# Attention and two expert layers in one kernel: q, k and w3 read from host-transposed copies, phi made for two heads at once

## The chip, the cores and the metric

The kernel runs on one core of a Trainium2 chip. The metric is the device time of one execution in microseconds (us), lower is better. Five engines take part: PE (matrix products and transposes; its weight loads are listed as PEld), DVE (vector operations, and the only one besides ACT that reads PE's results from PSUM here), ACT (activations and copies), POOL (GpSimd, elementwise on SBUF) and SP, which only issues DMAs. Each engine runs its instructions in a fixed order and waits on semaphores.

## The reference

```
scores = q @ k.T / sqrt(64), causal;  local = softmax(scores) @ v       # 2 x 8 heads, 576 tokens, D = 64
phi(x) = where(x > 0, x, exp(x) - 1) + 1
mem    = (phi(q) @ M_prev) / (phi(q) . z_prev + 1e-6)
x      = g * mem + (1 - g) * local,  g = sigmoid(beta) by head          # 1152 tokens x 512
h      = (x @ w1) * (x @ w2) @ w3;   x2 = h @ w_out                     # 512 -> 1024 -> 1024 -> 512
out    = sum over 4 experts e of p[:, e] * (relu(x2 @ e_w1[e]) @ e_w2[e])
```

The inputs w1, w2, w3 and w_out of the first layer are float64 and the rest float32.

## The kernel before

Every float32 operand of a product is split into a high part (rounded to 12 significant bits) and a low part (the rest), each carried by one float32r pass. Where nothing else is said a product takes three passes (`PASSES`, high-low, low-high, high-high). The high part is a copy (ACT `copy`, or `hi_pool` on POOL, L74), the low part a subtraction (`lo_pool` on POOL, L77, or `lo_dve` on DVE, L80).

The work has three parts in time. **Attention**: 16 heads in slots numbered from -1. In slot n the program emits stage z of head n+3, stage t of head n+2, stage a of head n+1 and stage b of head n, and between them "fills": the conversion of w_out, then W = w3 @ w_out in 16 units (`w_unit`, slots 3 to 10.5), then h of the first batch in 16 units (`b0`, slots 10.5 to 15), then its product with W (`c_unit`, slot 15). Each step has a place in its slot (`Z_AT`, `T_AT`, `A_AT`, `B_AT`), and a scheduler that knows modelled costs settles from this program the fixed order of each engine's instructions. **Second batch**: the same two products for the tokens of batch 1. **Experts**: four experts, each two products with a ReLU between them.

The stages of a head:

- z (`stage_z`): q, k and v lie with tokens on partitions, 5 tiles of up to 120 tokens. phi(q) is made (ACT `ex`, `phi`; DVE L165), multiplied by z and summed (DVE L169, L171), the norm is inverted and multiplied in (L173, L177). q, k, v and phi are each split on POOL into `qs`, `ks`, `vs`, `ps`, M into `ms`.
- t (`stage_t`): PE transposes `qs`, `ks` and `ps`, 15 transposes a head (L222, L229), ACT and DVE copy them out of PSUM to T = [(high; low), tokens] and pT (L223, L230, L231), and two DMAs (L232, L233) make `kTs`, which is k with the halves swapped, (low; high).
- a (`stage_a`): scores in two passes over 128 rows, [qh; ql] against [kl; kh] and against [kh; kl], then mask, row minimum and exponential (DVE L255, ACT L261), and the weights are scaled by the gate over the row sum (L300 to L306).
- b (`stage_b`): PE transposes the weights (`pt`, L341), ACT and DVE split them into `ph` and `pl`, and PE sums M's term (one pass, L359) and the products with v (L364).

For w3, `w_conv` turns 128 x 512 float64 words into float32 on ACT and DVE (`from64`, L100 to L105), and `w_trans` transposes the tile on PE (four transposes `w3p`, L425), copies the high part on ACT and subtracts the low part on DVE (`w3T`, L426, L427). All loads are issued by SP, in order.

## Time and profile before

| | before |
|---|---|
| device time, median of 3 runs | 798.97 us (798.64 to 801.09) |
| span of the profiled execution, first to last instruction | 798.1 us |
| PE busy | 750.8 us (94%), 4352 instructions |
| DVE busy | 396.9 us (50%), 838 instructions |
| ACT busy | 283.0 us (35%), 671 instructions |
| POOL busy | 354.5 us (44%), 423 instructions |
| DMA packets | 69176, of which 38272 under 512 B |

The span is the profile's own time; it leaves out what lies before the first and behind the last instruction, and is 0.9 us under the median of the runs. A share of busy time is an average over the three parts of the program, which have different limits, so the rows below are taken by part. "Idle before" is the time that an engine waited in front of a group, with the instruction whose end released it.

### The profile page before, as it was taken

How to read it: one execution, taken by the hardware profiler on the slowest of the kernel's cores; microseconds unless marked ns; L12 is line 12 of the kernel's file. 1: busy time of each engine (PE TensorE's matmuls, PEld its weight loads, DVE VectorE, ACT ScalarE, POOL GpSimd, SP SyncE). 2: the span in 40 equal slices, each digit the busy share in tenths (PEclk: the TensorE clock that was granted, in tenths of full speed). 3: DMA queues.
4: the chain of work that ended last, by engine and by line, in shares of the span. 5: the costliest groups of instructions: out<-in, count | busy, mean ns of one | idle time of the engine just before them, and what ended most of it. 6: DMA issues, size and time to landing. Idle time of an engine off the chain costs nothing.

```text
span 798.1 us, 11693 instructions
## 1 busy us (share of the span) xinstructions
PE 750.8 (94%) x4352; PEld 668.4 (84%) x4352; DVE 396.9 (50%) x838; ACT 283.0 (35%) x671; POOL 354.5 (44%) x423
## 2 busy tenths in 40 slices
PE   2698998999899999899999999999999999999997
PEld 2486887889898999799988988889888898888986
DVE  4998999899999953665321211212112122121211
ACT  3877777676675643344220101201012010020100
POOL 6889377478798526722392018500194001500000
PEclk9857999899999999999999999999999999999999
DMA  6554545444433322431141004200042000201010
GB/s 144 159 144 140 147 124 144 127 121 124 129 104 103 109 65 93 159 106 54 41 131 41 1 1 132 79 1 1 1 132 79 1 1 1 67 0 40 14 40 26
DMA packets 69176, 62.41 MB, mean 78 GB/s; under 512 B 38272, under 2 KB 54656, under 8 KB 69120
## 3 DMA queue, kind: packets, MB, share of 16 engines
q1 hardware_dynamic: 69120, 61.68, 27.3%
q8 instruction: 34, 0.56, 0.3%
q14 instruction: 22, 0.18, 0.1%
...
## 4 chain that ended last, share of the span: by engine, by line
PE 68%; DVE 12%; DMA 8%; POOL 7%; issue 3%; ACT 2%; SPq 0%; DVEq 0%; POOLq 0%; ACTq 0%
PE d L653 25%; PE o L670 25%; PE ab L488 5%; PE c L550 4%; DMA wr<-in_moe_w_dram 3%; PE wacc L434 2%; DMA wor<-in_moe_w_out_dram 2%; PE xv L364 2%; POOL P L306 2%; PE sc L252 2%; PE pt L341 2%; DVE tu L102 1%; DVE P L255 1%; DVE tf L105 1%; DMA w3r<-in_moe_w_dram 1%
## 5 line engine op out<-in xcount | busy, mean ns | idle before, releaser
L670 PE MATMUL o<-el,he 128*128 128x512 f32 x864 | 200.9, 392 | 0.0
L670 PEld LDWEIGHTS o<-el,he 128*128 128x128 f32 x864 | 161.8, 188 | 36.1
L659 ACT ACTIVATE he<-d 128x512 fp32r<-128x512 f32 (+2 forms) x96 | 47.2, 491 | 342.1 <-PE d L653 339.6
L74 POOL TENSOR_SCALAR el<-rel 128x512 fp32r<-128x512 f32 x64 | 40.3, 636 | 210.9 <-PE d L653 186.4
L660 DVE SCALAR_TENSOR_TENSOR he<-d,he 128x512 fp32r<-128x512 f32 (+2 forms) x96 | 53.4, 557 | 147.2 <-ACT he L659 147.2
L488 PE MATMUL ab<-xT,ws 128*128 128x288 f32 x768 | 115.6, 301 | 2.9 <-DVE asb L537 1.5
L653 PE MATMUL d<-x2b,el 128*128 128x384 f32 (+1 forms) x768 | 113.8, 309 | 0.0
L653 PEld LDWEIGHTS d<-x2b,el 128*128 128x128 f32 x768 | 113.2, 189 | 0.7
L488 PEld LDWEIGHTS ab<-xT,ws 128*128 128x128 f32 x768 | 107.4, 192 | 4.5 <-DVE W L80 0.9
L653 PE MATMUL d<-x2a,el 128*128 128x512 f32 x384 | 89.6, 394 | 0.0
L653 PEld LDWEIGHTS d<-x2a,el 128*128 128x128 f32 x384 | 72.0, 188 | 16.9
L77 POOL TENSOR_TENSOR el<-rel,el 128x512 fp32r<-128x512 f32 x64 | 83.0, 1311 | 1.6
L679 DVE SCALAR_TENSOR_TENSOR acc<-o,pr,acc 128x512 f32<-128x512 f32 x27 | 20.3, 751 | 125.3 <-PE o L670 125.3
L550 PE MATMUL c<-hT,W 128*128 128x288 f32 x384 | 57.2, 298 | 3.9 <-DVE hT L80 3.7
L306 POOL TENSOR_SCALAR P<-P,sm 120x120 f32<-120x120 f32 (+4 forms) x71 | 55.1, 790 | 9.0 <-DVE sm L301 9.0
L550 PEld LDWEIGHTS c<-hT,W 128*128 128x128 f32 x384 | 52.4, 188 | 5.1 <-DVE hT L80 4.7
L434 PE MATMUL wacc<-wo,w3T 128*128 128x512 f32 x192 | 54.8, 420 | 0.0
L261 ACT ACTIVATE P<-P,mn 120x120 f32<-120x120 f32 (+4 forms) x80 | 46.7, 585 | 13.4 <-DVE mn L255 13.2
L341 PE MATMUL pt<-identF,P 114*120 114x114 f32 (+1 forms) x240 | 42.7, 287 | 5.2 <-DVE pl L80 2.9
L434 PEld LDWEIGHTS wacc<-wo,w3T 128*128 128x128 f32 x192 | 36.6, 201 | 6.7
L252 PE MATMUL sc<-kTs,T 128*120 128x120 f32 (+2 forms) x96 | 35.6, 380 | 4.7 <-DMA kTs<-T 3.1
L80 DVE TENSOR_TENSOR pl<-pt,ph 120x456 fp32r<-120x456 f32 (+1 forms) x64 | 37.4, 596 | 1.8 <-ACT ph L345 1.7
(112 smaller groups left out, 1059.2 us busy)
## 6 DMA issues: line engine op xcount, KB each, us to landing
...
```

The source lines that it names most:

```text
L77: nc.gpsimd.tensor_sub(dst, src, r32(hi))
L252: nc.tensor.matmul(ps_ap, lhsT=T[:, 0, q0[i] : q0[i] + RP], rhs=rhs, start=(m == 0), stop=(m == 1))
L261: nc.scalar.activation(Pt[i], Pt[i], AF.Exp, bias=mn[:, i : i + 1], scale=-1.0, accum_out=sm[:, i : i + 1])
L306: nc.gpsimd.tensor_scalar(out=Pt[i], in0=Pt[i], scalar1=sm[:, i : i + 1], scalar2=1.0, op0=ALU.mult, op1=ALU.mult)
L341: nc.tensor.transpose(pt[:, o - c0 : o - c0 + rows[i]], Pt[i][0 : rows[i], q0[j] : q0[j] + RP], identF[0 : rows[i], 0 : rows[i]],)
L434: nc.tensor.matmul(wacc[t], lhsT=w3T[u][:, a, c * P : (c + 1) * P], rhs=wo[4 * g + c][:, bb, :], start=(g == 0 and c == 0 and x == 0), sto ...
L488: nc.tensor.matmul(ps[:, 0:HS], lhsT=self.ws[u][:, wi, kk, :], rhs=xT[b, kk][:, xi, a * HS : (a + 1) * HS], start=(n == 0), stop=(n == 3 * ...
L550: nc.tensor.matmul(st["ps"][:, 0:HS], lhsT=Wt[kk][:, wi, d * P : (d + 1) * P], rhs=hT[kk][:, xi, a * HS : (a + 1) * HS], start=(kk == 0 an ...
L653: nc.tensor.matmul(ps, lhsT=ew1[m // 4 * 4 + kk][:, wi, m % 4 * P : (m % 4 + 1) * P], rhs=rhs[:, xi, :], start=(n == 0), stop=(n == 3 * KD ...
L659: nc.scalar.activation(ht[:, 0, :], ps, AF.Relu)
L660: nc.vector.scalar_tensor_tensor(out=ht[:, 1, :], in0=ps, scalar=0.0, in1=r32(ht[:, 0, :]), op0=ALU.max, op1=ALU.subtract,)
L670: nc.tensor.matmul(po, lhsT=hs[kk][:, xi, tt * P : (tt + 1) * P], rhs=ew2[kk][:, wi, :], start=(n == 0), stop=(n == 3 * KF - 1),)
```

## The change

The host passes transposed copies of q, k and w3 (`qT`, `kT`, `moe_w3T`), and q itself as before for phi. `load_head` reads qT and kT twice each, into the upper and the lower 64 partitions. `stage_h` makes of them T = (qh; ql) and K = two tiles, (kh; kh) and (kl; kl): the high parts by ACT copies, the low parts by POOL subtractions. The scores are still two passes of 128 rows, T against (kl; kl) and T against (kh; kh). Stages z and t and the DMAs to `kTs` are gone, and a head is loaded one slot later than before.

phi is made for two heads at once (`stage_pa`, `stage_pb`) on 120 x 640 elements. The product with z moves from DVE to POOL. phi is transposed in float32, both heads side by side, in 5 transposes for two heads, and split after it, the high part by ACT and the low part by DVE. The split of M is padded with zeros to 128 rows, and M's term takes two passes (high and low of phi) where it took one.

w3's tiles are split straight after the conversion, the high part by ACT and the low part by POOL. In `b0` the high part of w1 and w2 moves from POOL to ACT. The scaling of the last tile of weights is on ACT for all heads, where POOL did 7 of 16. The diff, cut to its core:

```diff
-Z_AT = (0.01, 0.15, 0.4, 0.45, 0.6, 0.75, 0.77)
-T_AT = (0.05, 0.06, 0.07, 0.08)
+PA_AT = (0.03, 0.2, 0.45, 0.6)
+PB_AT = (0.12, 0.15, 0.72)
+H_AT = (0.02, 0.1, 0.14, 0.75)
...
+    ms2 = [A1.tile([P, 2, 2 * D], F32R, name=f"ms{i}") for i in range(2)]
+    for t in ms2:
+        nc.gpsimd.memset(r32(t), 0.0)
+    def load_pair(p):
+        b, h = divmod(2 * p, H)
+        qn = A1.tile([RP, NQ, 2, D], F32, tag="qn", name=f"qn{p}")
+        for x in range(2):
+            src = q[b, h + x]
+            nc.sync.dma_start(out=qn[:, :, x, :], in_=bass.AP(src.tensor, src.offset, [[D, RP], [R * D, NQ], [1, D]]))
+        z = A1.tile([P, 2 * D], F32, tag="z", name=f"z{p}")
+        nc.sync.dma_start(
+            out=z, in_=z_prev[b, h : h + 2].rearrange("h d -> (h d)").unsqueeze(0).to_broadcast([P, 2 * D])
+        )
+        mr = A1.tile([P, D], F32, tag="mr", name=f"mr{p}")
+        nc.sync.dma_start(out=mr, in_=M_prev[b, h : h + 2].rearrange("h d e -> (h d) e"))
+        pair_t[p] = {"q": qn, "z": z, "m": mr}
...
+        for nm, src in (("q", qT), ("k", kT)):
+            t = A1.tile([P, S], F32, tag=f"{nm}d", name=f"{nm}d{n}")
+            for x in range(2):
+                nc.sync.dma_start(out=t[x * D : (x + 1) * D, :], in_=src[b, h])
...
+        t = A2.tile([RP, NQ, D], F32, tag="vr", name=f"vr{n}")
+        x = v[b, h]
+        nc.sync.dma_start(out=t, in_=bass.AP(x.tensor, x.offset, [[D, RP], [R * D, NQ], [1, D]]))
+        raw_t[n] = (*ts, t)
...
+    def stage_pa(p):
+        if p >= B * H // 2:
+            return []
+        st = pair_t[p]
+        h = 2 * p % H
+        def phi_a():
+            st["ex"] = ex = st["q"]
+            st["phi"] = phi = A1.tile([RP, NQ, 2, D], F32, tag="phi", name=f"phi{p}")
+            nc.scalar.activation(phi, st["q"], AF.Relu)
+            nc.scalar.activation(ex, st["q"], AF.Exp)
+            nc.vector.scalar_tensor_tensor(out=phi, in0=ex, scalar=1.0, in1=phi, op0=ALU.min, op1=ALU.add)
+        def phi_b():
+            ex, phi = (st[x].rearrange("p n h d -> p n (h d)") for x in ("ex", "phi"))
+            nc.gpsimd.tensor_mul(ex, phi, st["z"][0:RP].unsqueeze(1).to_broadcast([RP, NQ, 2 * D]))
+            m = ms2[p % 2]
+            for x in range(2):
+                o = slice(x * D, (x + 1) * D)
+                hi_pool(m[o, x, 0:D], st["m"][o, :])
+                lo_pool(m[o, x, D:], st["m"][o, :], m[o, x, 0:D])
+        def phi_c():
+            st["nrm"] = nrm = A1.tile([RP, NQ, 2], F32, tag="nrm", name=f"nrm{p}")
+            nc.vector.reduce_sum(out=nrm, in_=st["ex"], axis=AX.X)
+            nc.vector.scalar_tensor_tensor(
+                out=nrm, in0=nrm, scalar=1e-6, in1=gm[0:RP, h : h + 2].unsqueeze(1).to_broadcast([RP, NQ, 2]),
+                op0=ALU.add, op1=ALU.mult,
+            )
+            nc.vector.reciprocal(nrm, nrm)
+        def phi_d():
+            phi = st["phi"]
+            nc.vector.tensor_mul(phi, phi, st["nrm"].unsqueeze(3).to_broadcast([RP, NQ, 2, D]))
+        return [*zip(PA_AT, (phi_a, phi_b, phi_c, phi_d))]
+    q0 = [R * i for i in range(NQ)]
+    widths = [x + RP for x in q0]
+    rows = [R] * (NQ - 1) + [RP]
+    def stage_pb(p):
+        if p >= B * H // 2:
+            return []
+        st = pair_t.pop(p)
+        pT = A2.tile([P, 2, S], F32R, tag="pT", name=f"pT{p}")
+        pT_t[2 * p] = pT_t[2 * p + 1] = pT
+        def trans(c0, c1):
+            def f():
+                t0, t1 = q0[c0], q0[c1 - 1] + rows[c1 - 1]
+                ps = psQ.tile([P, 512], F32, tag="Q", name=f"tp{c0}_{p}")[:, 0 : t1 - t0]
+                for c in range(c0, c1):
+                    w = rows[c]
+                    nc.tensor.transpose(
+                        ps[:, q0[c] - t0 : q0[c] - t0 + w], st["phi"][0:w, c].rearrange("p h d -> p (h d)"),
+                        identF[0:w, 0:w],
+                    )
+                nc.scalar.copy(pT[:, 0, t0:t1], ps)
+                lo_dve(pT[:, 1, t0:t1], ps, pT[:, 0, t0:t1])
+            return f
+        return [*zip(PB_AT, (trans(0, NQ - 1), trans(NQ - 1, NQ)))]
+    def stage_h(n):
+        if n >= B * H:
+            return []
+        qd, kd, vr = raw_t.pop(n)
+        T = A2.tile([P, S], F32R, tag="T", name=f"T{n}")
+        K = A2.tile([P, 2, S], F32R, tag="K", name=f"K{n}")
+        vs = A2.tile([RP, NQ, 2 * D], F32R, tag="vs", name=f"vs{n}")
+        split_t[n] = T, K, vs
+        def fq():
+            nc.scalar.copy(T, qd)
+            lo_pool(T[D : 2 * D, :], qd[D : 2 * D, :], T[D : 2 * D, :])
+        def fk():
+            nc.scalar.copy(K[:, 0, :], kd)
+            lo_pool(K[:, 1, :], kd, K[:, 0, :])
+        def fv():
+            hi_pool(vs[:, :, 0:D], vr)
+            lo_pool(vs[:, :, D:], vr, vs[:, :, 0:D])
+        def nothing():
+            pass
+        return [*zip(H_AT, (fk, fq, nothing, fv))]
...
-                rhs = T[:, 1, k0:k1] if m else kTs[:, k0:k1]
-                nc.tensor.matmul(ps_ap, lhsT=T[:, 0, q0[i] : q0[i] + RP], rhs=rhs, start=(m == 0), stop=(m == 1))
+                nc.tensor.matmul(
+                    ps_ap, lhsT=T[:, q0[i] : q0[i] + RP], rhs=K[:, 1 - m, k0:k1], start=(m == 0), stop=(m == 1)
+                )
...
-            nc.scalar.activation(sm, sm, AF.Identity, bias=gle[0:RP, h : h + 1], scale=gl[0:RP, h : h + 1])
+            nc.vector.tensor_scalar(
+                out=sm, in0=sm, scalar1=1e-9, scalar2=gl[0:RP, h : h + 1], op0=ALU.add, op1=ALU.mult
+            )
             nc.vector.reciprocal(sm, sm)
             for i in range(NQ):
-                if i == NQ - 1 and n <= H:
+                if i == NQ - 1:
...
+        Pt, vs = prob_t.pop(n)
+        pT, ms = pT_t.pop(n), ms2[n // 2 % 2][:, n % 2, :]
...
-                nc.tensor.matmul(xv, lhsT=ms, rhs=pT[:, a0:a1], start=True, stop=False)
+                for x in range(2):
+                    nc.tensor.matmul(xv, lhsT=ms, rhs=pT[:, x, a0:a1], start=(x == 0), stop=False)
...
-        steps = stage_z(n + 3) + stage_t(n + 2) + stage_a(n + 1)
+        steps = stage_h(n + 2) + stage_a(n + 1)
+        steps += stage_pa(n // 2 + 1) if n % 2 == 0 else stage_pb((n + 1) // 2)
...
+            out=r.rearrange("p c f two -> p c (f two)"),
+            in_=w3T[g * 512 : (g + 1) * 512, t * 2 * P : (t + 1) * 2 * P].rearrange("(c p) f -> p c f", p=P),
         )
...
-        ps = psM.tile([P, 512], F32, tag="M0", name=f"w3p{u}", bufs=1)
-        for c in range(4):
-            nc.tensor.transpose(ps[:, c * P : (c + 1) * P], f[:, c * P : (c + 1) * P], identF)
-        nc.scalar.copy(w3T[u][:, 0, :], ps)
-        lo_dve(w3T[u][:, 1, :], ps, w3T[u][:, 0, :])
+        f = from64(raw3.pop(u), pf, f"l3{u}")
+        w3s[u] = pf.tile([P, 2, 4, P], F32R, tag="ws", name=f"w3s{u}")
+        nc.scalar.copy(w3s[u][:, 0], f)
+        lo_pool(w3s[u][:, 1], f, w3s[u][:, 0])
...
+    load_pair(0)
...
-    for st, n in ((stage_z, 0), (stage_t, 0), (stage_z, 1)):
+    for st, n in ((stage_h, 0), (stage_pa, 0)):
...
-    b0 = BUnits(0, hi_pool, lo_dve)
+    b0 = BUnits(0, nc.scalar.copy, lo_dve)
...
-        if n + 4 < B * H:
-            load_head(n + 4)
+        if n + 3 < B * H:
+            load_head(n + 3)
+        if n % 2 == 1 and (n + 3) // 2 < B * H // 2:
+            load_pair((n + 3) // 2)
...
+    inputs["qT"] = inputs["q"].transpose(0, 1, 3, 2)
+    inputs["kT"] = inputs["k"].transpose(0, 1, 3, 2)
+    inputs["moe_w3T"] = inputs["moe_w3"].T```

On PE, at the start of the program (`tq`, `tk`, `tr`, `tp` are the transposes of q, k, their last 120 tokens and phi; `sc` the scores; the number behind a name tells tiles apart). Before:

```order
L222 MATMUL tq_192<-identR,qs_173 128x114 x4
L222 MATMUL tk_198<-identR,ks_176 128x114 x4
L229 MATMUL tr_204<-identR,qs_173 128x120
L229 MATMUL tr_204<-identR,ks_176 128x120
L229 MATMUL tr_204<-identR,ps_180 128x120
L222 MATMUL tp_212<-identR,ps_180 128x114 x4
L222 MATMUL tq_274<-identR,qs_228 128x114 x4
L222 MATMUL tk_280<-identR,ks_231 128x114 x4
L252 MATMUL sc_0_308<-kTs_191,T_189 120x120
L252 MATMUL sc_0_308<-T_189 120x120
```

and of the change, the same place:

```order
L273 MATMUL sc_0_219<-K_144,T_143 120x120 x2
L273 MATMUL sc_0_219<-K_144,T_143 120x234 x2
L273 MATMUL sc_0_228<-K_144,T_143 120x348 x2
L273 MATMUL sc_0_228<-K_144,T_143 120x64 x2
L273 MATMUL sc_0_236<-K_144,T_143 120x462 x2
L273 MATMUL sc_0_241<-K_144,T_143 120x512 x2
L223 MATMUL tp_0_208<-identF,phi_152 128x114 x4
L273 MATMUL sc_1_326<-K_194,T_193 120x120 x2
```

The 23 transposes that stood ahead of the first scores are gone, and the transposes of phi stand behind them.

On POOL, between the scaling of the weights of heads 4 and 5, where the units of W run (`xT` is the split of attention's result, `w3s` that of w3's tiles). Before:

```order
L77 TENSOR_TENSOR vs_903<-vr_550,vs_903 120x5x64
L74 TENSOR_SCALAR qs_1305<-qr_919 120x5x64
L74 TENSOR_SCALAR ks_1317<-kr_921 120x5x64
L74 TENSOR_SCALAR xT_1_71<-xraw_761 128x576
L77 TENSOR_TENSOR qs_1305<-qr_919,qs_1305 120x5x64
L77 TENSOR_TENSOR ks_1317<-kr_921,ks_1317 120x5x64
L77 TENSOR_TENSOR xT_1_71<-xraw_761,xT_1_71 128x576
L74 TENSOR_SCALAR ms_1165<-mr_744 128x64
L77 TENSOR_TENSOR ms_1165<-mr_744,ms_1165 128x64
L74 TENSOR_SCALAR ps_1350<-phi_1218 120x5x64
L77 TENSOR_TENSOR ps_1350<-phi_1218,ps_1350 120x5x64
```

and of the change, the same place:

```order
L79 TENSOR_TENSOR w3s_774<-tf_l_768,w3s_774 128x512
L79 TENSOR_TENSOR w3s_832<-tf_l_826,w3s_832 128x512
L76 TENSOR_SCALAR vs_742<-vr_583 120x5x64
L76 TENSOR_SCALAR xT_1_69<-xraw_597 128x576
L79 TENSOR_TENSOR vs_742<-vr_583,vs_742 120x5x64
L79 TENSOR_TENSOR xT_1_69<-xraw_597,xT_1_69 128x576
L76 TENSOR_SCALAR ms_106<-mr_1144 64x64
L79 TENSOR_TENSOR K_1147<-kd_957,K_1147 128x576
L79 TENSOR_TENSOR ms_106<-mr_1144,ms_106 64x64
L79 TENSOR_TENSOR T_1146<-qd_954,T_1146 64x576
L79 TENSOR_TENSOR w3s_900<-tf_l_894,w3s_900 128x512
L79 TENSOR_TENSOR w3s_951<-tf_l_945,w3s_951 128x512
```

The splits of q, k and phi have left POOL's order, and the low parts of q, k and four tiles of w3 stand in it, each a subtraction of two SBUF tiles.

## Rows read from the trace of the kernel before

**Rows 1.** Busy by stretch: start:end, length, PE, PEld, DVE, ACT, POOL busy (count), clock, DMA, GB/s.
```profile
0.00:20.00 20.00, 5.46 (x28) 4.35 (x29) 8.98 (x20) 7.51 (x16) 13.32 (x28) 1.00 0.66 144
20.00:71.00 51.00, 38.84 (x178) 31.07 (x177) 47.02 (x119) 40.09 (x100) 44.42 (x52) 0.72 0.60 162
71.00:178.00 107.00, 102.20 (x622) 88.60 (x621) 99.06 (x233) 78.49 (x190) 67.96 (x96) 0.94 0.47 127
178.00:278.00 100.00, 94.05 (x705) 90.33 (x704) 97.32 (x227) 66.25 (x174) 80.88 (x100) 0.97 0.40 113
278.00:300.00 22.00, 22.00 (x170) 22.00 (x169) 13.30 (x28) 9.84 (x23) 4.97 (x7) 1.00 0.24 73
300.00:394.00 94.00, 88.32 (x648) 86.15 (x647) 48.73 (x78) 33.70 (x74) 41.91 (x37) 1.00 0.27 88
394.00:798.00 404.00, 399.97 (x2014) 345.94 (x2012) 82.45 (x137) 47.16 (x96) 101.05 (x108) 1.00 0.14 41
```

**Rows 2.** DVE groups, 0 to 300 us: busy us, mean ns of one, idle before.
```profile
L80 DVE TENSOR_TENSOR w3T<-w3p,w3T 128x512 fp32r<-128x512 f32 x16 | 10.8, 675 | 1.2 <-ACT w3T L426 1.1
L169 DVE TENSOR_TENSOR ex<-phi,z 120x320 f32<-120x320 f32 x16 | 10.5, 657 | 1.7 <-DMA z<-in_z_prev_dram 1.6
L230 DVE CAST T<-tr 128x240 fp32r<-128x240 f32 x16 | 6.3, 392 | 3.1 <-PE tr L229 3.1
L231 DVE CAST pT<-tr 128x120 fp32r<-128x120 f32 x9 | 2.4, 268 | 0.0
L80 DVE TENSOR_TENSOR pl<-pt,ph 120x456 fp32r<-120x456 f32 (+1 forms) x64 | 37.4, 596 | 1.8 <-ACT ph L345 1.7
L173 DVE RECIPROCAL nrm<-nrm 120x5 f32<-120x5 f32 x16 | 2.9, 178 | 0.9 <-ACT nrm L172 0.9
```

**Rows 3.** Timeline of DVE, 163 to 171 us: start us, us.
```profile
163.77 0.68 DVE L102 SCALAR_TENSOR_TENSOR tu<-tf,tu 128x512 uint32<-128x512 uint32 x1
164.37 0.48 DVE L171 TENSOR_REDUCE nrm<-ex 120x5 f32<-120x320 f32 x1
...
168.67 1.54 DVE L102 SCALAR_TENSOR_TENSOR tu<-tf,tu 128x512 uint32<-128x512 uint32 x1
```

**Rows 4.** Timeline of POOL, 160 to 200 us.
```profile
168.23 1.44 POOL L77 TENSOR_TENSOR xT<-xraw,xT 128x576 fp32r<-128x576 f32 x1
```

**Rows 5.** Busy on tile qs, 0 to 300 us: PE, PEld, POOL, clock, DMA, GB/s.
```profile
0.00:300.00 300.00, 13.41 (x80) 10.23 (x80) 25.66 (x32) 0.92 0.47 125
```

**Rows 6.** The same for tile ks.
```profile
0.00:300.00 300.00, 12.99 (x80) 10.48 (x80) 27.55 (x32) 0.92 0.47 125
```

**Rows 7.** The same for tile ps.
```profile
0.00:300.00 300.00, 12.85 (x80) 9.79 (x80) 25.91 (x32) 0.92 0.47 125
```

**Rows 8.** POOL groups, 0 to 300 us.
```profile
L74 POOL TENSOR_SCALAR ws<-tf 128x512 fp32r<-128x512 f32 x16 | 12.2, 764 | 13.8 <-PE ab L488 5.2 <-DVE pl L80 4.4 <-PE tr L229 2.8
L77 POOL TENSOR_TENSOR wo<-tf_wo,wo 128x512 fp32r<-128x512 f32 x8 | 11.6, 1445 | 1.1 <-ACT wo L403 1.1
```

**Rows 9.** Timeline of PE at full clock, 86 to 91 us.
```profile
86.69 0.60 PE L425 MATMUL w3p<-identF,tf_l 128*128 128x128 f32 x4
87.05 2.32 PE L434 MATMUL wacc<-wo,w3T 128*128 128x512 f32 x9
89.21 0.45 PE L222 MATMUL tq<-identR,qs 114*128 114x114 f32 x4
89.50 0.59 PE L341 MATMUL pt<-identF,P 120*120 120x120 f32 x4
89.85 0.35 PE L364 MATMUL xv<-pl,vs 114*128 114x228 f32 x1
90.04 0.22 PE L364 MATMUL xv<-ph,vs 114*128 114x114 f32 x1
```

**Rows 10.** Busy by stretch around a fall of the clock, columns as in the first group.
```profile
136.00:140.00 4.00, 1.48 (x8) 1.19 (x8) 4.00 (x8) 2.38 (x6) 3.36 (x4) 0.74 0.45 91
140.00:144.00 4.00, 4.00 (x10) 3.12 (x10) 4.00 (x10) 1.62 (x4) 2.17 (x5) 0.50 0.75 203
```

More of the change, by code (lines that the diff above doesn't have):

```diff
@@ L42 @@
     w2: bass.AP,
-    w3: bass.AP,
+    w3T: bass.AP,
     w_out: bass.AP,
@@ L52 @@
     NT, DM = out.shape
-    w1, w2, w3, w_out = (t.bitcast(U32) for t in (w1, w2, w3, w_out))
-    DF = w3.shape[0]
+    w1, w2, w3T, w_out = (t.bitcast(U32) for t in (w1, w2, w3T, w_out))
+    DF = w3T.shape[0]
     E = e_w1.shape[0]
@@ L395 @@
     wo = [po.tile([P, 2, DM], F32R, tag=f"o{c}", name=f"wo{c}") for c in range(KF)]
[L396 removed]
+    raw3, w3s, wacc = {}, {}, {}
     def wo_unit(c):
```

110 lines of the change are left out of this document (13 added, 97 removed).

## The prediction

> **What bounds the kernel now.** I read first the busy time by stretch [rows 1], then DVE's groups [rows 2], then the order in time on DVE, POOL and PE around single instructions [rows 3, 4, 9], and last what POOL spends on the tiles that the change takes away [rows 5 to 8].
>
> The experts, 394 to 798 us, keep PE busy 400.0 of 404 us [rows 1], and the change touches nothing there. In the second batch, 300 to 394 us, PE is busy 88.3 of 94, and only its start moves. So all that can be won lies in the first 300 us. There the reader is to see two engines near their end at once: from 71 to 278 us DVE is busy 99.06 of 107 and 97.32 of 100 us, PE 102.2 and 94.05, while POOL has 67.96 and 80.88 and ACT 78.49 and 66.25. From 20 to 71 us DVE has 47.02 of 51 and POOL 44.42, and PE only 38.84 at a mean clock of 0.72. From 278 to 300 us PE alone is full (the products of h with W). A saving on PE alone would thus be held back by DVE, and the other way round. The change saves on both, so I cost each and take the smaller.
>
> **DVE, the first term.** Removed: the low part of w3T, 10.8 us, the product with z, 10.5, and the copies of the transposed tiles, 6.3 and 2.4 [rows 2], together 30.0. Added: the low part of the transposed phi, 8 times the mean of the same subtraction for the weights, 0.596 (456 columns), and 8 times 0.268 (120 columns): 6.9 us. The sum's gate on DVE is 16 operations on 5 elements, each as long as the reciprocal of that size, 0.178: 2.8 us. The norm's 16 reciprocals become 8 with 8 other small operations, which cancel. Net 20.3. Three operations on phi (minimum and sum, reduction, scaling) now do two heads at once, 24 launches fewer with the same elements: each is worth between 0 and 0.178; I take half, 2.1. Against that, durations overlap: the operation that starts at 163.77 lasts 0.68 and the next starts at 164.37, so 0.08 of each is not DVE's pace [rows 3]. 81 operations go and 32 come, so 49 times 0.08 = 3.9 comes off. DVE's net: 20.3 + 2.1 - 3.9 = 18.5 us, between 16.4 and 20.5 by the launches alone.
>
> **PE, the second term.** At full clock four float32r transposes take 0.29 us from start to start (89.21 to 89.50), four float32 ones 0.35 (89.50 to 89.85), and four of w3 0.36 (86.69 to 87.05) [rows 9]. Removed: 240 transposes of q, k and phi, 240 x 0.0725 = 17.4, and 16 x 0.36 = 5.8 for w3. Added: 40 float32 transposes of phi, 40 x 0.0875 = 3.5, and M's second pass, twice a head: 0.19 for 228 columns (89.85 to 90.04), and by columns 0.29 for 348, so 16 x 0.48 = 7.7. Net 23.2 - 11.2 = 12.0 us, more where the clock is low. The scores stay two passes of the same columns: nothing.
>
> **POOL, the cover.** Removed: 25.66, 27.55 and 25.91 us for the splits of q, k and phi [rows 5 to 7] and 12.2 for w1 and w2 [rows 8], 91.3 in 112 operations. Added, in 56: the low parts of q and k, 32 subtractions of 576 columns, each between 1.44 (the one in rows 4) and 1.63 (1.445 for 512 columns [rows 8], by columns); I take 1.5, since the row with the same width is the nearer: 48. The low parts of w3, 16 x 1.445 = 23.1, and the product with z, 8 x 1.81 (640 columns): 14.4. Sum 85.5, so POOL has some 6 us less in all. But it is not evenly spread. From 71 to 178 us, where W is made, 7.5 heads lose 4.94 each (79.1 over 16) and gain 3.9, and all of w3 comes in: 67.96 - 37 + 29 + 23 = 83 us, in a stretch that should shrink to 95. POOL there rises from 64% to 87% busy: it hides, with little cover left. If that cover fails, the low parts of w3 are late for PE, and behind them in POOL's order stand q and k of a later head, as the two pieces of POOL's order in the part on the change show.
>
> **ACT and SP.** ACT takes sixteen copies of w1 and w2, at most 0.764 each [rows 8], into a stretch where it is busy 66.25 of 100 [rows 1], so 78; the rest is exchanged in kind. Nothing. On SP 32 DMAs to kTs go, and the loads of a head become wider rows; the transfer share is 0.40 to 0.66 [rows 1]. The loads of qT and kT have one buffer, so each waits on SP for POOL's subtraction of the head before, and loads of w3 stand behind it. It is issued a slot (over 12 us) ahead of its use. Nothing, and at most what the slow rival below says.
>
> **The sum by stretch.** From 71 to 278 us, 207 us long, DVE saves w3T's 9.5 (10.8 less the overlaps) and of the remaining 9.0, 0.56 a head, some 11.5 heads: 16 us. PE saves there 11.5 x 0.39 + 5.8 = 10.3 of 196.25 busy us, so it could not end it before 186 us, that is 21 us of gain at most. DVE's 16 is the smaller, and PE would be 97% busy. I take off 3 for that and for POOL's thin cover: 13. From 0 to 71 us DVE saves 4.5 x 0.56 = 2.5, and POOL, with 57.7 us busy there, loses 34.6 (7 heads are split by then) and gains 23.4 (6 heads): 11. The gain lies between; DVE is the busier from 20 us on, so I take 5, nearer to it. The first scores also lose 23 transposes ahead of them; that is worth between 0 and the 11 us that DVE idles of the first 20. I add nothing, since DVE's next work there, the conversion of w_out, waits for loads that the change does not bring forward; the upper end lies within rival 2. From 278 us on: nothing. Sum 18 us, against a span of 798.1, which is 0.9 under the median of the runs; I keep that offset: **798.97 - 18 = 781 us**.
>
> **One rule against the change.** At 168.67 us a conversion on DVE took 1.54 us where the same took 0.68 at 163.77 [rows 3]; POOL had begun a subtraction of 1.44 us at 168.23 [rows 4]. So POOL's work is not free for DVE. The Trainium skill (SBUF — State Buffer, section "SBUF: two separate sides") states why: the two share a pair of SBUF ports, and whichever starts first holds it for its whole instruction. These two rows agree. By it, three kinds of long POOL operations are added whose holds DVE feels; whether the sum falls depends on how POOL's old operations held it. That is the first rival.
>
> **The rivals.**
> 1. *POOL holds DVE longer.* A DVE operation that meets a hold waits half of it on average. 112 removed operations with a mean of 0.82 and 56 new ones with 1.53 give 112 x 0.41 = 46 and 56 x 0.765 = 43, no difference; that speaks against. But if only subtractions and products hold, 48 of the removed count, 48 x 0.41 = 20 against 43, and if one in three meets a DVE operation that needs the ports, 8 us are lost: gain 10, 789 us. Chance 0.17.
> 2. *The waits go too.* PE waits now for the splits, the copies of transposes and kTs. If the gain is PE's 21 from 71 to 278 us and POOL's 11 before it, 32: 767 us. For it: the removed operations are those waited for. Against it: DVE's 16. Chance 0.15.
> 3. *Hidden.* The change may move the work and not the time, if the order that the scheduler fixed leaves the same waits under other names: 799 us, chance 0.04. Both full engines lose work, which speaks against.
> 4. *Slower: the scores wait for POOL.* q's and k's low parts stand in POOL's order behind the scaling of a head, its v and up to four tiles of w3. If they come late, PE runs dry. From 136 to 140 us PE was busy 1.48 of 4, and from 140 to 144 the granted clock was 0.50, that is 1.2 GHz [rows 10]: 2.5 us idle and 2 of work lost, 4.5 for each such gap. With the gain of 18, it is slower than before by a measurable amount from the fifth such gap on; at 8 of the 13 heads from head 3 on it costs 36: 817 us. Against it: the operands are made a slot ahead, and POOL is at 87%. Chance 0.08.
>
> **How the numbers follow.** The forecast has 0.56. Faster is the forecast with rivals 1 and 2, 0.88; the same, 0.04; slower, 0.08; the bound between them is 0.3%, about what a measurement of this kernel can tell from no change. The range reaches from just under rival 2, 766, to just over rival 1, 791, which leaves out rivals 3 and 4 and a little of the tails.
>
> **What would show it.** Right: the last stretch of experts starts near 376 us in place of 394 and has the same length; DVE busy in the first part falls by 16 to 21 us and PE still waits little; POOL is near 87% busy while W is made. Wrong: DVE's conversions (L102) lasting mostly near 1.54 us and not near 0.68 would show rival 1; long idle times of PE in front of the scores, released by POOL's subtractions, and a clock of 0.5 beyond 80 us would show rival 4; a start of the experts before 365 us, rival 2. The prediction is wrong if the time is outside 766 to 791.

## The result and the profile after

The change made the kernel slower by half a per cent: 802.6 us median (801.7 to 803.4, 7 runs) against 797.5 us (7 runs) for the kernel before, a ratio of 1.0052 [1.0033, 1.0070]. The profiled execution took 803.4 us, its span is 801.6. The forecast was 781. Busy time, share and instructions of each engine, from the page of the kernel after:

```profile
PE 739.9 (92%) x4120; PEld 655.6 (82%) x4120; DVE 397.8 (50%) x786; ACT 286.2 (36%) x639; POOL 354.3 (44%) x362
```

DVE has 52 instructions and POOL 61 fewer than before, and both are busy as long as before.

Busy time by stretch of the kernel after, columns as in [rows 1]:

```profile
0.00:20.00 20.00, 7.12 (x25) 5.63 (x25) 10.04 (x25) 11.18 (x23) 15.56 (x26) 1.00 0.76 195
20.00:71.00 51.00, 35.51 (x142) 29.43 (x142) 47.88 (x102) 36.68 (x86) 46.27 (x45) 0.64 0.51 147
71.00:178.00 107.00, 89.90 (x453) 75.12 (x453) 95.51 (x194) 73.46 (x164) 87.83 (x86) 0.88 0.49 141
178.00:278.00 100.00, 93.83 (x657) 88.61 (x656) 96.82 (x225) 74.36 (x178) 54.46 (x58) 0.97 0.36 111
278.00:300.00 22.00, 21.07 (x161) 20.61 (x161) 14.73 (x29) 9.15 (x19) 6.35 (x6) 1.00 0.29 92
```

From 71 to 178 us, where W is made, DVE did 39 instructions fewer than before [rows 1], and was still busy 95.5 of 107 us; POOL rose from 68.0 to 87.8, and PE fell from 102.2 to 89.9 at a clock of 0.88 where it was 0.94. The two kernels are not at the same point of their work in a stretch, so this alone proves little; the reading is that PE got less to do and waited more, and that DVE got fewer instructions that lasted longer. The groups of DVE's instructions, kept apart by shape, first of the kernel after, 0 to 310 us (busy, mean ns of one, idle before):

```profile
L102 DVE SCALAR_TENSOR_TENSOR tu_wo<-tf_wo,tu_wo 128x512 uint32<-128x512 uint32 x8 | 11.6, 1451 | 1.5 <-ACT tf_wo L100 1.4
L102 DVE SCALAR_TENSOR_TENSOR tu_l<-tf_l,tu_l 128x512 uint32<-128x512 uint32 x16 | 16.7, 1042 | 0.0
L82 DVE TENSOR_TENSOR pl<-pt,ph 120x456 fp32r<-120x456 f32 x16 | 10.0, 624 | 1.6 <-ACT ph L371 1.5
L323 DVE TENSOR_SCALAR sm<-sm,gl 120x5 f32<-120x5 f32 x16 | 5.9, 372 | 0.0
L193 DVE SCALAR_TENSOR_TENSOR nrm<-nrm,gm 120x10 f32<-120x10 f32 x8 | 4.7, 589 | 0.1
```

and of the kernel before, the first three:

```profile
L102 DVE SCALAR_TENSOR_TENSOR tu_wo<-tf_wo,tu_wo 128x512 uint32<-128x512 uint32 x8 | 6.8, 855 | 0.0
L102 DVE SCALAR_TENSOR_TENSOR tu_l<-tf_l,tu_l 128x512 uint32<-128x512 uint32 x16 | 13.1, 821 | 0.3 <-ACT tf_l L100 0.3
L80 DVE TENSOR_TENSOR pl<-pt,ph 120x456 fp32r<-120x456 f32 x16 | 9.9, 617 | 0.0
```

These two conversions, which read and write SBUF alone, went from 0.86 and 0.82 to 1.45 and 1.04 us. They are the worst case: the other four conversions with two inputs (L102 and L105) changed by -0.02 to +0.30 us. The subtraction `pl`, which reads PE's transposes from PSUM, did not move (0.617, 0.624). An operation on 10 elements takes 0.59 us on average. The timelines say what the long ones lie beside. DVE of the kernel after, start and duration in us:

```profile
61.85 3.38 DVE L102 SCALAR_TENSOR_TENSOR tu_wo<-tf_wo,tu_wo 128x512 uint32<-128x512 uint32 x1
...
65.61 1.36 DVE L193 SCALAR_TENSOR_TENSOR nrm<-nrm,gm 120x10 f32<-120x10 f32 x1
```

and POOL at the same time:

```profile
60.68 1.27 POOL L79 TENSOR_TENSOR wo<-tf_wo,wo 128x512 fp32r<-128x512 f32 x1
61.92 1.40 POOL L79 TENSOR_TENSOR xT<-xraw,xT 128x576 fp32r<-128x576 f32 x1
63.28 1.40 POOL L79 TENSOR_TENSOR K<-kd,K 128x576 fp32r<-128x576 f32 x1
64.64 0.76 POOL L79 TENSOR_TENSOR ms<-mr,ms 64x64 fp32r<-64x64 f32 x1
65.48 1.47 POOL L79 TENSOR_TENSOR T<-qd,T 64x576 fp32r<-64x576 f32 x1
```

DVE's conversion begins inside POOL's first subtraction and ends 0.55 us after the third; undisturbed it takes some 0.67. It waited not for one POOL instruction but for three that stood back to back. The next one on POOL, `ms`, lasts 0.76 us here, where the shortest of its 16 take 0.31. The 10-element operation begins in POOL's subtraction for T and ends with it.

The work that the change gives POOL, 0 to 310 us of the kernel after (`qn` is the product with z):

```profile
L79 POOL TENSOR_TENSOR K<-kd,K 128x576 fp32r<-128x576 f32 x16 | 26.3, 1642 | 9.7 <-ACT K L248 9.4
L79 POOL TENSOR_TENSOR T<-qd,T 64x576 fp32r<-64x576 f32 x16 | 25.2, 1574 | 4.1 <-ACT T L244 3.1
L79 POOL TENSOR_TENSOR w3s<-tf_l,w3s 128x512 fp32r<-128x512 f32 x16 | 21.8, 1364 | 9.3 <-ACT w3s L448 9.1
L183 POOL TENSOR_TENSOR qn<-phi,z 120x640 f32<-120x640 f32 x8 | 13.0, 1619 | 0.3
```

PE's longest waits in the kernel after, 0 to 310 us (total, times, longest), and then those of the kernel before:

```profile
PE sc L273 <- POOL K L79: 10.9, 3, 8.5
PE tp L223 <- DVE phi L201: 8.2, 3, 3.9
PE wacc L456 <- DVE W L82: 6.3, 3, 3.6
PE sc L273 <- DVE mn L278: 5.7, 4, 3.5
```

```profile
PE tq L222 <- POOL qs L77: 5.9, 1, 5.9
PE tp L222 <- DVE pT L231: 4.7, 4, 1.7
PE xv L359 <- DVE mn L255: 3.8, 4, 2.5
PE sc L252 <- DMA kTs<-T: 3.1, 5, 1.8
```

The waits of 8.5 and 5.9 us are those for the first head, at the start of the program.

**Splitting DVE's time.** To compare kernels, I take from the timeline every DVE instruction that starts up to the last `xraw` (the end of attention, which the same work has to reach in every kernel). Its undisturbed duration is the 10th percentile of all instructions of the same operation, shape and source memory (PSUM or SBUF) over the eighteen profiles of this study. The sum of these is DVE's *own work*; what the instructions last beyond it is the *lengthening*; *idle* is what remains of the time to the end of attention. Durations of successive instructions overlap, so own work, lengthening and idle together exceed the end by 37 to 43 us. Each row is one profiled execution, and executions of one kernel differ by some us (801.7 to 803.4 for the change, 788.5 to 796.4 for e2), so 2 or 3 us between rows say little. All in us:

| kernel | ratio to before [95%] | end of attention | own work | lengthening | idle |
|---|---|---|---|---|---|
| before | 1 | 301.6 | 265.8 | 41.8 | 35.2 |
| after | 1.0052 [1.0033, 1.0070] | 305.5 | 245.4 | 57.7 | 39.6 |
| e1, w3 part alone | 1.0157 [1.0123, 1.0191] | 315.1 | 255.5 | 51.4 | 49.4 |
| e2, all but the w3 part | 0.9942 [0.9919, 0.9966] | 297.4 | 256.8 | 48.3 | 32.7 |
| e3, w3's low parts on DVE | 1.0024 [1.0005, 1.0042] | 301.0 | 256.1 | 53.3 | 31.5 |
| e4, places moved by 0.01 | 1.0061 [1.0035, 1.0088] | 306.4 | 246.0 | 59.9 | 38.4 |
| e5, two banks for wacc | 1.0039 [1.0017, 1.0061] | 302.2 | 246.1 | 63.2 | 32.0 |
| e8, e2 with phi times z on DVE | 1.0073 [1.0057, 1.0089] | 305.9 | 263.2 | 48.7 | 34.8 |
| e9, e1 with low parts on DVE | 1.0036 [1.0017, 1.0055] | 300.2 | 265.3 | 43.0 | 34.5 |
| e10, q, k low: one-input | 0.9969 [0.9945, 0.9992] | 296.8 | 247.2 | 46.4 | 42.9 |
| e11, e2 with extra two-input | 1.0147 [1.0114, 1.0179] | 313.0 | 257.1 | 55.8 | 40.7 |
| e12, e2 with extra one-input | 1.0183 [1.0153, 1.0212] | 317.4 | 257.6 | 62.4 | 38.5 |
| e13, no w3 low parts | 0.9999 [0.9978, 1.0021] | 300.3 | 246.7 | 57.6 | 35.0 |
| e14, no low parts of w3, q, k | 0.9813 [0.9784, 0.9841] | 288.1 | 246.4 | 28.6 | 50.1 |

The first two rows are the result: DVE's own work falls by 20.4 us, its instructions last 15.9 us longer, and it idles 4.4 us more. These three cancel to 0.1 us. That attention still ends 3.9 us later is the overlaps: with 52 instructions fewer, 4.0 us of overlap between successive ones are gone (41.2 before, 37.2 after).

### The profile page after: what moved, and what is told of

It reads as the page before. It is cut to its first block, busy times and chain, and to the rows that moved or that the text cites. A ratio compares the mean times of both kernels' runs of the same rounds, so it can differ in the third digit from the quotient of the medians.

```text
span 801.6 us, 11092 instructions
## 1 busy us (share of the span) xinstructions
PE 739.9 (92%) x4120; PEld 655.6 (82%) x4120; DVE 397.8 (50%) x786; ACT 286.2 (36%) x639; POOL 354.3 (44%) x362
## 4 chain that ended last, share of the span: by engine, by line
PE 63%; DVE 17%; POOL 6%; DMA 6%; issue 5%; ACT 3%; SPq 0%; DVEq 0%; POOLq 0%; ACTq 0%
PE d L673 25%; PE o L690 25%; PE ab L508 4%; PE c L568 4%; PE wacc L456 2%; DMA wr<-in_moe_w_dram 2%; DVE tu L102 2%; DMA w3r<-in_moe_w3T_dram 2%; DVE tf L105 2%; DVE P L278 2%; POOL P L331 2%; DVE pl L82 2%; PE xv L391 1%; DMA qd<-in_qT_dram 1%; PE pt L367 1%
## 5 line engine op out<-in xcount | busy, mean ns | idle before, releaser
L76 POOL TENSOR_SCALAR el<-rel 128x512 fp32r<-128x512 f32 x64 | 40.4, 636 | 210.8 <-PE d L673 187.8
L673 PEld LDWEIGHTS d<-x2a,el 128*128 128x128 f32 x384 | 72.1, 188 | 16.7
L79 POOL TENSOR_TENSOR el<-rel,el 128x512 fp32r<-128x512 f32 x64 | 83.5, 1319 | 1.6
L273 PE MATMUL sc<-K,T 128*120 128x120 f32 (+2 forms) x192 | 49.7, 382 | 18.4 <-POOL K L79 10.9
L456 PE MATMUL wacc<-wo,w3s 128*128 128x512 f32 x192 | 55.4, 439 | 6.3 <-DVE W L82 6.3
L331 POOL TENSOR_SCALAR P<-P,sm 120x120 f32<-120x120 f32 (+1 forms) x64 | 48.8, 778 | 20.6 <-DVE sm L326 13.2
L273 PEld LDWEIGHTS sc<-K,T 128*120 128x120 f32 x192 | 34.6, 225 | 23.9 <-POOL K L79 11.4
L456 PEld LDWEIGHTS wacc<-wo,w3s 128*128 128x128 f32 x192 | 40.0, 215 | 15.4 <-DVE W L82 7.0
```

The costliest lines, as they stand in the source:

```text
L79: nc.gpsimd.tensor_sub(dst, src, r32(hi))
L273: nc.tensor.matmul(ps_ap, lhsT=T[:, q0[i] : q0[i] + RP], rhs=K[:, 1 - m, k0:k1], start=(m == 0), stop=(m == 1))
L331: nc.gpsimd.tensor_scalar(out=Pt[i], in0=Pt[i], scalar1=sm[:, i : i + 1], scalar2=1.0, op0=ALU.mult, op1=ALU.mult)
L456: nc.tensor.matmul(wacc[t], lhsT=w3s[u][:, a, c, :], rhs=wo[4 * g + c][:, bb, :], start=(g == 0 and c == 0 and x == 0), stop=(g == 1 and c ...
L673: nc.tensor.matmul(ps, lhsT=ew1[m // 4 * 4 + kk][:, wi, m % 4 * P : (m % 4 + 1) * P], rhs=rhs[:, xi, :], start=(n == 0), stop=(n == 3 * KD ...
```

## The experiments

The theories at the start: **H**, POOL's new two-input instructions hold up DVE's instructions on SBUF; **L**, what POOL makes comes late, because its queue is fuller, and PE and then DVE wait; **O**, an accident of the order that the scheduler laid out.

### The two halves of the change, the place of w3's low parts, and shifted places (e1 to e4)

e1 is the kernel before with w3 read transposed and its low parts on POOL, nothing else of the change. e2 is the change with w3 as before. e3 is the change with

```diff
-        lo_pool(w3s[u][:, 1], f, w3s[u][:, 0])
+        lo_dve(w3s[u][:, 1], f, w3s[u][:, 0])
```

and e4 the change with every place of `A_AT` later by 0.01 of a slot.

> The kernel before with the w3 part of the change alone (w3 read transposed, low part on POOL). Theory H (POOL's new two-input instructions hold the SBUF ports that DVE needs, so DVE's saving is paid back in longer DVE instructions): the 9.5 us that DVE saves are mostly eaten, 793 to 798 us, and the conversions of w3 on DVE (tu_l, now 0.821 us) last 0.95 or more. Rival L (holds are small, what was lost is lateness of q's and k's low parts): the w3 part gives its gain, 786 to 790 us, tu_l stays under 0.88.

> The change without its w3 part (w3 transposed on PE and split on ACT and DVE as before). H: DVE gets w3T's 10.8 us back but 22 us of POOL holds go, 798 to 804 us, no clear difference from the change; tu_l back near 0.82 us. Rival L: the tiles of w3 no longer stand ahead of q's and k's low parts on POOL, the waits of PE for POOL fall, 785 to 793 us. If w3's part was a real gain inside the change: 808 us or more.

> The change with w3's low part on DVE in place of POOL. H: DVE takes 16 subtractions (some 0.7 us each, 11 us) and loses 22 us of holds by POOL; 796 to 804 us, DVE's tu_l under 0.95 us. If DVE's own work is what counts and holds do not: 810 to 814 us. Rival L: PE's waits for POOL fall, 790 to 796 us.

> The change with the places of stage a shifted by 0.01 of a slot, a control for how much the order that the scheduler settles is worth by itself; all instructions are the same. H and L: within 2.4 us of the change, 800 to 805 us. Rival O (the time is decided by the accidents of the order): more than 4 us off on either side.

Measured: e1 810.7 us, e2 792.7, e3 799.2, e4 802.9. The w3 part alone loses 1.6%, the rest alone wins 0.6%: e2 is faster than both kernels. e1 lies above both of its ranges (793 to 798 and 786 to 790), and its `tu_l`, 0.885 us, between the values that H and L gave; e2 lies in L's range and not in H's, e3 in H's.

e4 does not test O. In its trace PE, DVE, ACT and POOL each do the same instructions in the same order as in the change: the shift did not reach the order, and e4 is the change measured once more (1.0052, 1.0061). So O has no test of its own. What comes nearest is e5 below, where DVE's order agrees with that of the change, place by place, in 417 of 786 instructions, and the ratio is 1.0039.

In e1 DVE does 10 us less of its own work; 9.6 come back as lengthening, and 14 us of idle time are new. DVE waits longer for the scores in e1 than in the kernel before. Two of its waits of e1, 0 to 310 us, and then that for the scores in the kernel before:

```profile
DVE P L255 <- PE sc L252: 8.6, 6, 4.9
DVE tu_l L102 <- ACT tf_l L100: 3.3, 2, 2.8
```

```profile
DVE P L255 <- PE sc L252: 4.1, 4, 2.0
```

With w3's low parts on DVE (e3) the idle time falls by 8 and the lengthening by 4, while the own work rises by 10.7, so most of it is given back. Each of the 16 low parts is no longer what it was before, either: the old one read PSUM and took 0.675 us [rows 2], the new one reads SBUF. DVE's group in e3:

```profile
L82 DVE TENSOR_TENSOR w3s<-tf_l,w3s 128x512 fp32r<-128x512 f32 x16 | 16.1, 1004 | 0.0
```

### Waits inside the w3 part (e5 to e7)

e5 lets the accumulator alternate between two banks, e6 moves the conversion of a slice of w3 back by one product (from behind the last product of unit u-1 to behind the first of unit u, for u+1), e7 is e6 with the low parts on DVE.

```diff
-            wacc[t] = psM.tile([P, 512], F32, tag="M1", name=f"wacc{t}", bufs=1)
+            wacc[t] = psM.tile([P, 512], F32, tag=f"M{t % 2}", name=f"wacc{t}", bufs=1)
```

> The change with one edit: the accumulator of the product w3 times w_out takes PSUM banks M0 and M1 in turn, where it took M1 alone. In the change PE waits 6.3 us in three places to begin the next accumulator until DVE has written the low part of the one before (longest 3.6). Theory K (the bank makes w3's part lose): those waits go and the time falls by 4 to 6.5, to 796 to 798.5. Theory B (the buffer of the converted w3 slices: ACT's cast waits on PE and stands before the rest of ACT's and POOL's queue) and theory H (POOL's low parts hold DVE's instructions up): PE only waits somewhere else, 801 to 804 as the change's 802.6.

> The change with one edit: a slice of w3 is converted after the first product of the unit before it, three products ahead of its use, where the change converts it four products ahead, right behind the last product that reads the buffer it needs. In the change ACT waits 8.1 us for that buffer and POOL 9.1 us for ACT's cast. Theory B: both waits go, and with them the lateness of everything queued behind; 793 to 797. Theory K: nothing of PE's wait for the bank changes, 801 to 804. Theory H: POOL's low parts are the same, DVE's conversions stay near 1.04 and 0.92 us each, 801 to 804. If three products are too little, PE waits for w3s instead and the time rises to 805 or more.

> The change with both: slices of w3 converted one product later, and their low parts on DVE (that alone took 799.2). Theory B: the waits for the buffer go here too, 792 to 796. Theory H alone: as with the low parts on DVE alone, 797.5 to 801, since nothing that POOL holds is moved. If DVE is the bound of this stretch, its 16 us for the low parts stay and the time stays at 799.

Measured: e5 799.0, e6 802.4, e7 800.1 us, with ratios of 1.0039, 1.0082 and 1.0058. In e5 the wait is gone, and PE's first wait while W is made is now POOL's (70 to 190 us):

```profile
PE wacc L456 <- POOL w3s L79: 5.6, 5, 1.9
```

The ratio only went from 1.0052 to 1.0039, inside the intervals, and 799.0 lies between the range of theory K and that of the others: a gain from the second bank is not shown. In e6 ACT still waits for PE before it may write w3s (6.1 us from 70 to 190 us, 8.1 in the change), and the W tiles are finished within some 1.1 us of where they were: the scheduler laid the moved step almost where it had been. e7 is e3 itself: PE, DVE, ACT and POOL do the same instructions in the same order. Yet e3 has 1.0024 [1.0005, 1.0042] and e7, measured at another time, 1.0058 [1.0036, 1.0080], so ratios of separate measurements can stand 0.34% apart without a cause in the program. So these two leave theory B untested; a third buffer for w3s wasn't tried.

### The product with z (e8)

```diff
-            nc.gpsimd.tensor_mul(ex, phi, st["z"][0:RP].unsqueeze(1).to_broadcast([RP, NQ, 2 * D]))
+            nc.vector.tensor_mul(ex, phi, st["z"][0:RP].unsqueeze(1).to_broadcast([RP, NQ, 2 * D]))
```

> The change without its w3 part (792.7) with one more edit: the product of phi with z goes back from POOL to DVE, for two heads at once. POOL is rid of 8 instructions of 1.62 us (13 us), DVE gets 8 of 640 elements, by the row of the 640-element product with the norm (1.0 to 1.15 us) 8 to 9 us more. Theory H (POOL's two-input instructions make DVE's last longer by about what they take themselves): DVE's other instructions shorten by 8 to 13 us, so the two about cancel, 789 to 793. Theory L (POOL's lateness limits): POOL's low parts of K, T and P come earlier by up to 1.6 us a pair, 788 to 791. If DVE alone is the bound and holds are nothing: 8 more, of which about two thirds on the path, 797 to 799.

Measured: 801.8 us, above all three ranges and 9 above e2 by the medians, about what its 8 instructions take on DVE (9.0 us busy). H had said that the two would cancel; the lengthening did not move (48.3, 48.7), though POOL had 13 us less of two-input work. So this one move to POOL is worth its full time. That fits DVE being the bound here. It is not shown, for the product also stands in the chain that makes phi: of the 8.5 us by which attention ends later, 6.4 are own work and 2.1 idle time.

### w3 alone once more, POOL's kinds of instruction, and extra ones (e9 to e12)

e9 is e1 with the low parts on DVE. e10 is the change with

```diff
-            lo_pool(K[:, 1, :], kd, K[:, 0, :])
+            for _ in range(2):
+                hi_pool(K[:, 1, :], kd)
```

and the same for T, so that the subtraction is left out and the high part written in its place, twice. e11 and e12 are e2 with this in `run_slot`, twice a head; e11 has `lo_pool(spare, mask[:, 0:320], mask[:, 0:320])` as its body:

```diff
+    def extra():
+        for _ in range(2):
+            hi_pool(spare, mask[:, 0:320])
```

> The kernel before with the w3 part alone, as in the run that took 810.7, but w3's low parts on DVE in place of POOL. In that run DVE did 10 us less of its own work up to the end of attention (every instruction counted at the duration that it has undisturbed), its instructions lasted 10 us longer than that, and it idled 14 us more, waiting for work that POOL's queue had made late. Theory L (POOL's lateness): DVE gets 10.8 us of work back (16 of 0.67), some 4 of the lengthening go, and the 14 us of idle time go: 800 to 805. If the lost transposes on PE or w3's new loads are what hurts, the idle time stays and the work comes on top: 812 or more. If it is only the lengthening of DVE's instructions: near 811 again, since 4 less and 10.8 more of work meet the idle time.

> The change, but POOL's subtractions for the low parts of q and k (32 of 1.6 us, two inputs) are each replaced by two one-input multiplications by one that write the high value in their place: the subtraction is left out. Theory H (only POOL's two-input instructions hold DVE's SBUF instructions up): POOL is about as busy as before, but the lengthening of DVE's instructions, 58 us in the change up to the end of attention, falls to 42 to 48, and the time by 7 to 11, to 791 to 796. Theory L (POOL's time and lateness, whatever the kind): POOL's time is nearly the same, so 800 to 804. If any POOL instruction holds DVE up: the lengthening stays near 58 and the time at 800 to 804.

> The change without its w3 part (792.7), with two more POOL subtractions a head, 32 in all, of 320 columns on a spare tile that nobody reads: two inputs each, some 0.85 us by columns from the 1.5 us for 576, 27 us of POOL. Theory H: DVE's instructions lengthen by a third of that time, as they do by 49 us for 118 us of two-input POOL work in the run without them: 8 to 11 us, and the time rises by 5 to 9, to 798 to 802. Theory L: by POOL's queue alone, the same as the run beside it with one-input instructions. If POOL's spare time hides them: 791 to 794.

> As the run beside it, but each added subtraction is two multiplications by one of the same 320 columns, one input each, so that POOL is busy about as long. Theory H: one-input instructions hold DVE up by a quarter as much or less; DVE lengthens by 1 to 4 us, the time is 793 to 797, and lower than with the two-input ones. Theory L: the same time as with the two-input ones within 2 us. If POOL's spare time hides them: 791 to 794.

Measured: e9 799.2, e10 794.7, e11 808.7, e12 812.3 us. e9 against e1: the low parts leave POOL, DVE gets its 9.8 us of work back, and 14.9 us of idle time and 8.4 of lengthening go. So it is the low parts on POOL that made e1 slow, and not the lost transposes or the new loads (799.2 lies just under the 800 to 805 of L). With the low parts on DVE the w3 part is worth nothing: DVE's own work is that of before, and the 64 transposes that PE is rid of were not what bound it.

e10 is what H forecast: POOL's instructions for T and K take 52.9 us in place of 51.5, and yet the lengthening falls by 11 us and the time by 8. (The copies also no longer wait for ACT's high part, which they do not read; that may have a share.) e11 and e12 stand against H in its pure form: POOL's groups, 0 to 300 us, of e11 and then of e12,

```profile
L79 POOL TENSOR_TENSOR spare<-mask 128x320 fp32r<-128x320 f32 x32 | 28.5, 889 | 1.1
```

```profile
L76 POOL TENSOR_SCALAR spare<-mask 128x320 fp32r<-128x320 f32 x64 | 38.7, 605 | 2.6
```

cost 16 and 19.6 us, 0.56 and 0.51 for each us that POOL is loaded with, whatever the kind; H had 5 to 9 and under 5, and both were missed. L had the two within 2 us of each other; they are 3.6 apart, with POOL loaded 10 us more in e12. Nobody reads the spare tile, so all of this is through POOL's queue and its holds, or through the order, which the scheduler laid out anew. The scheduler put the extra instructions early (the last at 129 and 151 us). There POOL is 65 to 91% busy in e2, so this price is that of a crowded stretch.

e12 also shows that one-input instructions are not harmless. Its lengthening rises by 14.1 us, that of e11 by 7.5. The longest DVE instruction of e12, and POOL at that time:

```profile
38.05 5.33 DVE L101 TENSOR_SCALAR tu_wo<-wor 128x512 uint32<-128x512 uint32 x1
```

```profile
37.45 0.85 POOL L79 TENSOR_TENSOR ms<-mr,ms 64x64 fp32r<-64x64 f32 x1
38.27 0.45 POOL L76 TENSOR_SCALAR spare<-mask 128x320 fp32r<-128x320 f32 x1
38.70 1.26 POOL L79 TENSOR_TENSOR wo<-tf_wo,wo 128x512 fp32r<-128x512 f32 x1
39.92 1.52 POOL L189 TENSOR_TENSOR qn<-phi,z 120x640 f32<-120x640 f32 x1
41.42 0.45 POOL L76 TENSOR_SCALAR spare<-mask 128x320 fp32r<-128x320 f32 x1
41.84 1.25 POOL L79 TENSOR_TENSOR wo<-tf_wo,wo 128x512 fp32r<-128x512 f32 x1
```

An instruction that takes some 0.41 us undisturbed lasts until the sixth POOL instruction of a row has ended, and two of these six are the added one-input copies.

### Without the low parts (e13, e14), and less on POOL (e15, e16)

e13 leaves w3's low parts out (PE takes the high part in their place), e14 those of q and k too. e15 and e16 are e2 with the high part of v, or of x, copied by ACT in place of POOL.

> The change with w3's low parts left out: POOL does not make them and PE takes the high part in their place, in the same number of products. POOL is rid of 16 subtractions, 21.8 us; nothing else changes. Theory L (POOL's queue is what the other engines wait for, at about half a us for each us that it is loaded with, as the runs with extra instructions gave: 16 us for 28.5 and 19.6 for 38.7): 11 to 12 us less, 789 to 793. Theory H (only the lengthening of DVE's instructions counts, a third of POOL's two-input time): 5 less, 796 to 798.5. If POOL hides it: 801 to 804.

> The change with the low parts of w3, q and k all left out: POOL is rid of 48 subtractions, 73 us; PE takes high parts in their place, in as many products. If what the change saves on DVE and PE was sized right and POOL's new work ate it, the time is that of the prediction's sum or below it: 766 to 783. If DVE's or PE's saving was not there to begin with, it stays at 786 or more. DVE's own work up to the end of attention stays at 245 us either way; its lengthening, 58 us, should fall to 25 to 35, a third of 73 less.

> The change without its w3 part (792.7), with the high part of v (16 copies, 9.3 us on POOL) on ACT. Theory L at half a us for each: 4 to 5 less, 787 to 789.5. If ACT, some 72% busy in this stretch, becomes late instead: 793 to 798. If neither counts: 791 to 794.

> The change without its w3 part (792.7), with the high part of x (8 copies, 5.9 us on POOL) on ACT. Theory L: 3 less, 788 to 791. If these copies wait on POOL for DVE anyway (23.8 us idle before them in that run) and their removal frees nothing: 791 to 794. If ACT becomes late: 794 to 797.

Measured: e13 797.8, e14 783.1, e15 801.2, e16 793.8 us. e14 is the one that decides. It computes with as many products and as much DVE work as the change, only POOL lacks 73 us of subtractions and nobody waits for them, and it takes 783.1 us, 19.6 below the change, 15 below the kernel before, 2 above the forecast. The lengthening halves, from 57.7 to 28.6. That the forecast is met so closely is partly luck: POOL has less to do in e14 than in the kernel before (41.7 against 68.0 us from 71 to 178 us), so that the lengthening is 13.2 us below that of before, while DVE idles 14.9 us more. Its stretches from 20 us on:

```profile
20.00:71.00 51.00, 36.85 (x152) 31.33 (x153) 43.29 (x101) 35.57 (x81) 33.65 (x37) 0.64 0.60 163
71.00:178.00 107.00, 94.06 (x509) 80.24 (x508) 89.93 (x208) 77.71 (x175) 41.65 (x53) 0.93 0.51 149
178.00:278.00 100.00, 96.34 (x711) 92.75 (x710) 92.04 (x228) 74.80 (x179) 48.14 (x55) 0.98 0.37 115
```

Against the change, from 71 to 178 us, DVE does 208 instructions in 89.9 us in place of 194 in 95.5, and PE 509 in place of 453. Two of the DVE groups that stood above, in e14:

```profile
L102 DVE SCALAR_TENSOR_TENSOR tu_wo<-tf_wo,tu_wo 128x512 uint32<-128x512 uint32 x8 | 6.8, 854 | 0.2 <-ACT tf_wo L100 0.2
L193 DVE SCALAR_TENSOR_TENSOR nrm<-nrm,gm 120x10 f32<-120x10 f32 x8 | 1.8, 219 | 0.0
```

The 10-element operation lasts 0.22 us here, and `tu_wo` at what it was before. e13 lies in the range that H gave, but came there by the other way: the lengthening stayed (57.6) and the idle time fell by 4.6. e15 is slower than e2 and above all its ranges: POOL now waits for ACT before v's low part, in 0 to 300 us

```profile
L79 POOL TENSOR_TENSOR vs<-vr,vs 120x320 fp32r<-120x320 f32 x16 | 16.6, 1037 | 31.5 <-ACT vs L252 31.4
```

so relief of POOL is no gain if its next instruction then waits for a busy engine. e16 (0.9973) is not to be told from e2, and L's 788 to 791 was missed. **The best version is e2**, the change without its w3 part, 0.9942 [0.9919, 0.9966] of the kernel before; its gain is not quite twice the 0.34% that lie between e3 and e7.

## Why the prediction was wrong

- **DVE, the first term: right, at its lower end.** Forecast were 22.4 us of work less 3.9 for overlaps, 18.5 net, between 16.4 and 20.5. DVE's own work fell by 20.4 and the overlaps by 4.0, 16.4 net.
- **The small operations** were taken at 0.178 each, or left to cancel. They took 0.372 and 0.589. Undisturbed they take 0.21 and 0.15, and without the low parts 0.291 and 0.219, so the rest is lengthening.
- **PE, the second term: the count right, and not the bound.** Instructions fell from 4352 to 4120, the 232 that the prediction's terms give. With this saving PE waited more, not less: its granted clock from 71 to 178 us fell from 0.94 to 0.88, and its four longest kinds of wait up to 310 us, shown above, are 31 us together where the kernel before has 17.5.
- **POOL, the cover: the size right, the price wrong.** K 26.3, T 25.2, w3s 21.8 and the product with z 13.0 (shown above) make 86.3 us where 85.5 were forecast, and POOL's 87.8 of 107 us while W is made (82%) is near the 83 of 95 (87%). But "it hides, with little cover left" is the step that failed. In the sum stood 3 us off for PE's limit and POOL's thin cover together; measured are 15.9 of lengthening and 4.4 of idle time. The sum weighed POOL's busy time, some 6 us less in all, and left its kind to rival 1: up to the end of attention POOL's two-input work rose from 98.7 to 138.2 us and its one-input work fell from 118.5 to 75.4. Where low parts leave POOL, the time falls: by 11.5 us from e1 to e9, 4.8 from the change to e13, 19.6 to e14.
- **0 to 71 us: 5 us of gain did not come.** POOL was to lose 11 us there; it went from 57.7 [rows 1] to 61.8. The first two pairs of heads came 11 us earlier (POOL began to split their x at 59.5 and 91.2 in place of 70.7 and 102.4), so POOL did more of the later heads' work. W came later: the last conversion of w_out on POOL, for which it waits, began at 68.9 in place of 65.2, its first tile was finished at 98.3 in place of 84.9 and its last at 187.7 in place of 179.0. By then the heads' lead was gone (fourth pair 171.8, before 167.5). The reading, which no run tests, is that what was saved went into work that nobody waited for yet.
- **Rival 1 (POOL holds DVE longer) had the mechanism and the wrong size**: 8 us. It let one in three of the operations meet a hold and wait half of one. In the trace, up to the end of attention, 76 of DVE's subtractions, conversions and products that read SBUF alone lay beside a two-input POOL instruction in the kernel before and lasted 0.37 us longer than undisturbed, 28.5 us; in the kernel after 98 by 0.50, 49.1 us. Beside one-input POOL instructions alone it was 0.09 and 0.07 each, and beside none under 0.01. So both factors grew, and the holds of POOL instructions in a row add up, as the 3.38 us show. Of the places named in advance, L102 has a mean of 1.45 for w_out, 1.04 for w3 and 0.93 for w1 and w2, between 1.54 and 0.68.
- **Rival 4 (the scores wait for POOL)** spoke of heads from 3 on, and there it did not happen: of the 10.9 us of `sc` behind `K`, 8.5 are the wait for head 0, and 0.2 and 2.1 those of heads 1 and 2 (at 17.5 and 28.5 us). **Rival 3** gave nearly the measured time, 799, for a reason that the runs do not support: work did go, and came back as longer instructions. That is luck.
- **The experts** start at 397 us where 376 was forecast; in e14 they start at 378.
- **The rule against the change** (Trainium skill, "SBUF — State Buffer", section "SBUF: two separate sides") speaks of one pair of ports, which a POOL instruction that starts first keeps from a DVE instruction with two SBUF inputs for its whole length. The lengthening agrees: 0.50 us beside two-input POOL instructions in the kernel after. In all the lengthening grew by 15.9 us, so rival 1, at 8, was the right mechanism at half its size.

Open: how the loss of a single load divides between holds and lateness. e10 and e14 acted through the lengthening (in both DVE's idle time rose), e13 through idle time, e11 and e12 through both, and taking the product with z off POOL (e8) through neither. Open too is what the scheduler's new order has to do with each of these results, for no run changed the order alone.
